# A retention, two mixtures of experts: rows normalised in two pieces, steps of a choice and of an early part placed anew

## The chip, the cores and the metric

The kernel runs on one core of a Trainium2 chip. A core has TensorE (PE, matrix products), VectorE (DVE), ScalarE (ACT) and GpSimd (POOL), SyncE (SP) that issues transfers, and 16 DMA engines. Each engine works through its own instructions in order and waits on semaphores of the others. The metric is the time of one execution on the device in microseconds, as a median of several runs.

## The reference

Three parts follow one another. The first is a causal retention of 8 batches, 8 heads, 576 positions, 64 columns; its output is read as 4608 rows of 512 columns. The second and the third send each row to one of 8 experts of two layers.

```python
scores = scale * np.matmul(q, k.transpose(0, 1, 3, 2))
Dmat = np.where(rel >= 0, gamma[:, None, None] ** rel[None, :, :], 0.0)
x = np.matmul(scores * Dmat[None], v)        # (8, 8, 576, 64), then 4608 rows of 512
...
# first mixture: each row to its best expert, times the gate's probability
expert_idx = np.argmax(x @ w_gate, axis=1)
h = np.maximum(xe @ w1[e], 0.0)              # 512 -> 1024
out[mask] = gate_w[mask, None] * (h @ w2[e]) # 1024 -> 512
...
# second mixture: the pairs (row, expert) by falling logit; a pair is taken
# if its row is free and its expert has fewer than 576 rows
for idx in np.argsort(-flat):
    tok, e = (int(idx) // E, int(idx) % E)
    if assigned[tok] >= 0 or counts[e] >= cap:
        continue
    assigned[tok] = e
    counts[e] += 1
```

## The kernel before, in words

A float32 product is made of float16 products: an operand is split into a high and a low half (w1h and w1l, hh and hl, the two halves of xhl), and three products of halves are summed.

**Attention** (`attention`, L137) goes through 36 row tiles, one in a step, and a list of stages that each step runs for tiles at different offsets. In a step POOL makes qz and vf from the loads of q and v, TensorE makes transposed copies, scores pS and outputs pO, DVE multiplies (s, xT), ACT copies out of PSUM. The small tiles lg, mx, ge, m, OH are the gate's choice for a group of four tiles. Two helper generators are advanced between the stages: `early` at two possible places of a step (`EARLY` lists the pairs of step and place), and `onward`, which holds the setup of later stages; for steps 10 to 17 that is `select_setup` (L1312), in which POOL makes jf and DVE five fsteps out of it.

**early** (L836) prepares the first three row tiles of expert 0 while attention still runs. In its pieces it makes tables, a list, gathers the three tiles (POOL, w2h<-Xs,ix, into a buffer that later holds weights), then for each tile: ACT's Square with a sum into scA, DVE's normaliser on that sum, ACT's Copy with the scale (high half), DVE's low half (w2l<-w2h,scA,w2l), and a transposition issued by SP (xT<-w2l). The first layer of expert 0 starts on these.

**The first mixture** (`moe1`, L1020) runs the experts one after another: `layer1` makes ph in PSUM, ACT evicts hh (L620) and DVE hl (L621), `layer2` makes py. While one expert runs, `prep(e)` (L1042) prepares another in pieces: tables and list, gathers (xg), and for each row tile `normalise` (L550) and `turn`, which issues the transposition xT<-xhl. `normalise` is Square on ACT (L544, or on DVE for expert 0's own rest), the normaliser's three small DVE instructions on sc (L401 to L403), Copy on ACT (L557) and low on DVE (L560). The tile xhl has three buffers. `mixed` advances a piece when the layer has made a given number of matmul calls: `P0`, `N1` and `N6` list these numbers for expert 0, for most of the others and for expert 6, and a dict at L1211 those of expert 0's rest layer. The matmuls, Square and Copy are kept in the order in which they are written; the small DVE instructions follow a scheduler.

**The second mixture** (`moe2`) first makes a choice for each expert: `choose` (L1556) goes through digits of a threshold (cnt, any, dig), then sums what was taken (s on DVE L1615, its matmul L1618), then the base (V, L1670 and L1681) and the list (G, L653 to L655, L676). A choice runs beside the layers of experts chosen earlier. After each of its steps a budget of nanoseconds of matmul columns must have passed before the next one is written; `PACE` holds the budgets for the choices from the fourth on, `FIRST` and `SECOND` those of the first three. From the list follow the gathers xg<-X1s and the transpositions xT<-xg.

Of the kernel before, what the change touches and what calls it, by code (L numbers as in the profile page):

```python
# [9 lines left out]
F32 = mybir.dt.float32  # L10
F16 = mybir.dt.float16
# [5 lines left out]
W = 514  # L17
# [8 lines left out]
TA = 26  # L26
SA = 3
LEAD_IN = 6
CAST = (4, 3)
EARLY = ((28, 1), (29, 0), (29, 1), (30, 0), (30, 1), (32, 0), (32, 1), (33, 0), (33, 1), (34, 0), (34, 1), (35, 0))  # L30
POOL_STORES = 29
AT_GATHER = 30
T0 = (76, 88)
LATE = 4
SOON = 3
P0 = (1, 19, 30, 68, 80)
RANK = (32, 40, 48)
N1 = (14, 82, 102, 122, 142, 170)
LOGITS = (96, 99, 101, 105, 109)
N6 = (30, 50, 70, 90, 108)  # L40
G6 = (102, 114, 184)
G7 = (50, 62, 98, 122, 146, 170)
R = 5
NONE = -1.0e30
LEAD = 2
PACE = dict(key=7000, cnt=3000, any=2000, dig=1800, sum=3300, base=4000, list=3000)
SECOND = dict(key=4000, cnt=2500, any=1700, dig=1500, sum=2600, base=3000, list=2600)
FIRST = dict(key=3000, cnt=1700, any=1200, dig=800, sum=1900, base=3400, list=2600)
ASIDE = dict(key=7500, base=3500, list=4000)
# [485 lines left out]
def scale2(k, x, sc, q, dve=False, pin=False):  # L535

    nc = k.nc
    if dve:
        q = k.fp.tile([128, 512], mybir.dt.bfloat16, name="sq", bufs=1)
        d = nc.vector.scalar_tensor_tensor(q, x, 1.0, x, op0=OP.mult, op1=OP.mult, accum_out=sc[:, 0:1])  # L540
        if pin:
            pe(k, d)
    else:
        d = nc.scalar.activation(q.bitcast(mybir.dt.bfloat16), x, AF.Square, accum_out=sc[:, 0:1])  # L544
        if pin:
            pe(k, d)
    normalizer(nc, sc[:, 0:1], sc[:, 1:2], sc[:, 2:3])


def normalise(k, xg, dve=False, to=None, pin=False):  # L550


    nc = k.nc
    h, sc = to or (k.fp.tile([128, 1024], F16, name="xhl", bufs=3), k.fp.tile([128, 6], F32, name="sc", bufs=12))
    x = xg[:, :512]
    scale2(k, x, sc, h[:, 0:512], dve, pin)
    d = nc.scalar.activation(h[:, 0:512], x, AF.Copy, scale=sc[:, 1:2])  # L557
    if pin:
        pe(k, d)
    nc.vector.scalar_tensor_tensor(h[:, 512:1024], x, sc[:, 1:2], h[:, 0:512], op0=OP.mult, op1=OP.subtract)  # L560
    nc.vector.tensor_scalar(sc[:, 3:4], sc[:, 2:3], 2.0 ** -14, None, op0=OP.mult)
    k.copied = nc.gpsimd.tensor_copy(sc[:, 4:6], xg[:, 512:514])
    return h, sc
# [272 lines left out]
def early(k, X):  # L836


    nc = k.nc
    k.nA = k.cp.tile([128, 4], F32, name="nA")  # L840
    OA = k.OH[:, 0, 0:TA]
    inc = k.lp.tile([128, TA], F16, name="incA", bufs=1)
    nc.vector.tensor_tensor_scan(inc, k.one_h[:, 0:TA], OA, 0.0, op0=OP.mult, op1=OP.add)
    yield
    pb = k.tp([128, 2])
    nc.tensor.matmul(pb[:, 0:1], k.lt_h, inc[:, TA - 1:TA], start=True, stop=True)
    nc.tensor.matmul(pb[:, 1:2], k.one_h, inc[:, TA - 1:TA], start=True, stop=True)
    nc.vector.tensor_copy(k.nA[:, 0:2], pb)
    nc.vector.tensor_tensor(k.nA[:, 2:3], k.nA[:, 0:1], inc[:, TA - 1:TA], op=OP.add)
    nc.vector.tensor_scalar(k.nA[:, 3:4], k.nA[:, 0:1], -1.0, 128.0 * SA, op0=OP.mult, op1=OP.add)  # L850
    yield
    V = k.lp.tile([128, 1, TA + 4], F16, name="VA", bufs=1)
    tables(k, V, TA, inc[:, None, :], k.nA[:, 0:1])
    nc.vector.scalar_tensor_tensor(OA, inc, k.nA[:, 3:4], OA, op0=OP.is_gt, op1=OP.mult)
    begun = cover(k, V[:, 0, :], TA, k.nA[:, 0:1], k.nA[:, 2:3], 128 * SA)
    yield
    ix, _ = lists(k, V[:, 0, :], TA, k.nA[:, 0:1], k.nA[:, 2:3], SA, k.slot, begun=begun)

    yield
    g = k.wp.tile([128, 8, 512], F16, name="w2h").rearrange("p f d -> p (f d)").bitcast(F32)  # L860
    h = k.wp.tile([128, 8, 512], F16, name="w2l").rearrange("p f d -> p (f d)")
    sc = k.cp.tile([128, SA, 6], F32, name="scA")
    rows = [gather(k, X[0:128 * TA, :], ix[:, s:s + 1], xg=g[:, W * s:W * (s + 1)])[:, 0:512] for s in range(SA)]
    to = [h[:, 1024 * s:1024 * (s + 1)] for s in range(SA)]
    k.early = new_xT(k), [sc[:, s, :] for s in range(SA)]

    def square(s):
        nc.scalar.activation(to[s][:, 0:512].bitcast(mybir.dt.bfloat16), rows[s], AF.Square, accum_out=sc[:, s, 0:1])

    def scaled(s):  # L870
        nc.scalar.activation(to[s][:, 0:512], rows[s], AF.Copy, scale=sc[:, s, 1:2])

    def low(s):
        nc.vector.scalar_tensor_tensor(to[s][:, 512:1024], rows[s], sc[:, s, 1:2], to[s][:, 0:512], op0=OP.mult, op1=OP.subtract)
        turn(k, to[s], k.early[0], s)
        nc.gpsimd.tensor_copy(sc[:, s, 4:6], g[:, W * s + 512:W * (s + 1)])

    for s in range(SA):
        yield
        square(s)  # L880
    yield
    normalizer(nc, sc[:, :, 0], sc[:, :, 1], sc[:, :, 2])
    nc.vector.tensor_scalar(sc[:, :, 3], sc[:, :, 2], 2.0 ** -14, None, op0=OP.mult)
    yield
    scaled(0)
    scaled(1)
    yield
    low(0)
    scaled(2)
    yield  # L890
    low(1)
    low(2)


# [121 lines left out]
def moe1(k, X, X1, w1, w2):  # L1016
    nc = k.nc
    X1v = X1.rearrange("(t p) c -> p t c", p=128)
    rows, scales, xTs = {}, {}, {}
    small = lambda e: CAPS[e] == CAP2  # L1020
# [21 lines left out]
    def prep(e):  # L1042

        s0 = 0 if e else SA
        if e == 0:
            yield from moe1_tables(k)
        else:
            xTs[e], scales[e] = new_xT(k), []
        at = args(e)
        n = tiles(e) - s0  # L1050
        begun = cover(*at, CAP2 if small(e) else 128 * n)
        yield
        ix, _ = lists(*at, n, k.slot2 if small(e) else k.slot, small(e), begun=begun)
        rows[e] = [gather(k, X, ix[:, s:s + 1]) for s in range(n)]
        for s in range(n):
            yield
            x, sc = normalise(k, rows[e][s], not e, pin=True)
            turn(k, x, xTs[e], s0 + s, 64 if s == 4 and small(e) else 128)
            scales[e].append(sc)
        for sc in scales[e]:  # L1060
            k.tc.keep_in_program_order(nc.vector.tensor_tensor(sc[:, 0:1], sc[:, 3:4], sc[:, 4:5], op=OP.mult))

# [63 lines left out]
    x1, g, hs, ws, gates = None, {}, {}, {}, {}  # L1126
    for e in range(8):
        w = ws[e] = k.w[e]
        steps = {}
# [43 lines left out]
        to = None  # L1173
# [39 lines left out]
        if e < 6:  # L1213
            x1 = columns(e)
            for s in (4, 0, 1, 2, 3) if small(e) else range(tiles(e)):
                at = {8: load}
                if s == SA and e == 0:
                    steps = {40: load, 20: lambda: next(p1, None), 60: lambda: next(p1, None)}
                    mixed(layer1(k, xTs[0], w, CAP1, to=hs[0], spans=[[(128 * SA, CAPS[0] - 128 * SA)]]), steps)
                if s == (3 if small(e) or e == 5 else tiles(e) - 1) and e < 6:  # L1220
                    ahead = prep(e + 2)
# [90 lines left out]
def select_setup(k):  # L1312
# [36 lines left out]
    for n in range(R):  # L1349
        if n in (2, 4):  # L1350
            yield
        nc.gpsimd.memset(k.f.ones[:, n], 16.0 ** -(n + 1))
        nc.vector.tensor_scalar(k.f.step[:, n], jf, 16.0 ** -(n + 1), None, op0=OP.mult)
    yield
    nc.gpsimd.memset(k.f.ones[0:1], 0.0)
    k.one_f = p.tile([1, 128], F32, name="one_f")
    nc.gpsimd.memset(k.one_f, 1.0)
# [637 lines left out]
```

## Time and profile before

| | us |
|---|---|
| median of three runs | 1047.06 (1047.06 to 1047.94) |
| the profiled execution | 1046.41 |
| its span, first to last instruction | 1044.5 |
| TensorE busy | 998.0 (96%) |
| VectorE busy | 617.6 (59%) |
| ScalarE busy | 441.6 (42%) |
| GpSimd busy | 331.4 (32%) |

Mean granted clock of TensorE over the span: 0.994 of full speed. Attention ends near 194 us, the first mixture near 620, the second's products near 1030; what is behind that are the last stores.

In the timeline a line holds the start, the duration, the engine, the line of the kernel, the operation, what it writes and reads, how many instructions were merged (x3), and in brackets how long the engine had stood idle before and which engine's work released it. L123 is a helper that records all of attention's instructions, so there one goes by the names of tiles. A wait for several semaphores is put down to the one that came last.

### The profile page before, as it was taken

The numbers are of one execution on the slowest core, as the hardware profiler recorded it, in microseconds if no ns is written. First come the engines' busy times: TensorE is split into PE (matmuls) and PEld (weight loads), VectorE is DVE, ScalarE is ACT, GpSimd is POOL, SyncE is SP. The second block draws the span as 40 slices with busy tenths as digits, with TensorE's granted clock in tenths as the row PEclk, the third lists the DMA queues.
The fourth block names the chain that finished last, engine by engine and source line by source line (L and its number), as shares of the span: only waits on it lengthen the run. The fifth ranks groups of instructions, "written<-read, shape, count | busy, mean of one in ns | idle before, by whom it ended". The sixth has DMA issues, their size and how long they took to land.

```text
span 1044.5 us, 23410 instructions
## 1 busy us (share of the span) xinstructions
PE 998.0 (96%) x9165; PEld 665.9 (64%) x9165; DVE 617.6 (59%) x1648; ACT 441.6 (42%) x814; POOL 331.4 (32%) x588
## 2 busy tenths in 40 slices
PE   6999999899999999999999999999999999999994
PEld 5887887556666657565676446474747474757662
DVE  2557767786866566567743676585648475624230
ACT  3556656564545455446521253233223232423330
POOL 6665656431130203030410241523032424313101
PEclk9999999999999999999999999999999999999998
DMA  9899995698887787779972261848274646745510
GB/s 218 204 250 259 236 266 139 155 250 181 203 235 153 213 168 201 175 200 241 197 137 35 72 209 35 231 149 208 77 158 147 153 161 159 215 142 161 142 37 33
DMA packets 276791, 177.65 MB, mean 170 GB/s; under 512 B 201968, under 2 KB 244736, under 8 KB 276672
## 3 DMA queue, kind: packets, MB, share of 16 engines
q1 hardware_dynamic: 264848, 139.22, 55.8%
q0 software_dynamic: 11680, 36.59, 10.8%
q8 instruction: 74, 1.21, 0.5%
q14 instruction: 45, 0.37, 0.1%
q10 hardware_dynamic: 144, 0.26, 0.1%
HBM read 116.83 MB, written 31.02 MB: 142 GB/s over the span
## 4 chain that ended last, share of the span: by engine, by line
PE 71%; DVE 8%; DMA 6%; issue 6%; POOL 4%; ACT 2%; SPq 1%; POOLq 0%; ACTq 0%; DVEq 0%
PE py L641 32%; PE ph L615 28%; PE tp L123 3%; DMA xg<-Xs,ix 2%; PE py L637 2%; PE pO L123 2%; PE pS L123 1%; DMA v<-in_v_dram 1%; POOL vf L123 1%; SPq L123 1%; DVE hl L621 1%; DVE w2l L499 1%; POOL qz L123 1%; DVE w1l L499 1%; DMA xT<-xhl 1%
## 5 line engine op out<-in xcount | busy, mean ns | idle before, releaser
L615 PE MATMUL ph<-xT,w1h 128*128 128x288 f16 (+6 forms) x2048 | 355.4, 289 | 10.7 <-DVE sc L401 3.4
L615 PEld LDWEIGHTS <-w1h 128*128 128x128 f16 x2048 | 195.3, 98 | 69.8 <-issue 15.1
L615 PE MATMUL ph<-xT,w1l 128*128 128x288 f16 (+6 forms) x1024 | 224.7, 289 | 0.0
L641 PE MATMUL py<-w2h,hh 128*128 128x512 f16 x512 | 194.2, 379 | 0.0
L641 PE MATMUL py<-w2h,hl 128*128 128x512 f16 x512 | 194.2, 379 | 0.0
L641 PE MATMUL py<-w2l,hh 128*128 128x512 f16 x512 | 194.1, 379 | 0.0
L641 PEld LDWEIGHTS <-hh 128*128 128x128 f16 x1024 | 98.3, 98 | 109.0 <-issue 0.4
L620 ACT ACTIVATE hh<-ph 128x576 f16<-128x576 f32 (+6 forms) x136 | 80.8, 594 | 171.1 <-PE ph L615 159.6
L621 DVE SCALAR_TENSOR_TENSOR hl<-ph,hh 128x576 f16<-128x576 f32 (+6 forms) x136 | 93.8, 690 | 58.6 <-ACT hh L620 51.7
L615 PEld LDWEIGHTS <-w1l 128*128 128x128 f16 x1024 | 99.6, 98 | 28.2 <-issue 1.7
L499 DVE SCALAR_TENSOR_TENSOR w1l<-stage,w1h 128x1024 f16<-128x1024 f32 x60 | 73.0, 1221 | 41.7 <-ACT w1h L496 40.5
L641 PEld LDWEIGHTS <-hl 128*128 128x128 f16 x512 | 50.1, 98 | 55.9
L499 DVE SCALAR_TENSOR_TENSOR w2l<-stage,w2h 128x1024 f16<-128x1024 f32 x64 | 78.4, 1226 | 8.6 <-ACT w2h L496 8.0
L530 POOL DMA_INDIRECT xg<-X1s,ix x40 | 45.4, 1135 | 107.1 <-DVE ix L685 56.8
L123 DVE TENSOR_TENSOR s<-pS,ct 128x512 f32<-128x512 f32 x72 | 46.4, 686 | 44.7 <-PE pS L123 44.5
L496 ACT ACTIVATE w2h<-stage 128x1024 f16<-128x1024 f32 x64 | 66.8, 1047 | 0.0
L496 ACT ACTIVATE w1h<-stage 128x1024 f16<-128x1024 f32 x60 | 62.2, 1047 | 0.9 <-DMA stage<-in_moe_w_dram 0.9
L544 ACT ACTIVATE x1r<-py 128x512 bf16<-128x512 f32 x37 | 22.0, 596 | 95.5 <-PE py L641 61.3
L698 POOL TENSOR_TENSOR x1r<-nm,sc 128x1 f32<-128x1 f32 x34 | 6.4, 189 | 175.0 <-DVE nm L403 172.6
L123 POOL TENSOR_TENSOR xTl<-xT,xTh 128x512 f16<-128x512 f32 x34 | 39.5, 1163 | 60.6 <-ACT xTh L123 55.5
L530 POOL DMA_INDIRECT xg<-Xs,ix x36 | 41.5, 1152 | 41.2 <-DVE ix L685 25.8
L1775 POOL DMA_INDIRECT out_dram<-w2T,ti x20 | 22.5, 1125 | 92.6 <-ACT w2T L1774 58.7
(399 smaller groups left out, 1507.5 us busy)
## 6 DMA issues: line engine op xcount, KB each, us to landing
stage<-in_moe_w_dram SPq DMA_DIRECT2D x128, 512.0 KB
q<-in_q_dram SPq DMA_DIRECT2D x64, 128.0 KB
k<-in_k_dram SPq DMA_DIRECT2D x32, 256.0 KB
v<-in_v_dram SPq DMA_DIRECT2D x32, 256.0 KB
X1s<-x1r SPq DMA_DIRECT2D x28, 257.0 KB
Xs<-xr SPq DMA_DIRECT2D x5, 1028.0 KB
Xs<-xr POOLq DMA_DIRECT2D x3, 771.0 KB
Xs<-xr POOLq DMA_DIRECT2D x1, 1028.0 KB
```

The lines of the kernel that those rows point to most:

```text
L123: return lambda *args, **kw: self.tc.keep_in_program_order(f(*args, **kw))
L496: d = nc.scalar.activation(at(h, i), t, AF.Copy, scale=128.0)
L499: d = nc.vector.scalar_tensor_tensor(at(l, i), t, 128.0, at(h, i), op0=OP.mult, op1=OP.subtract)
L530: nc.gpsimd.indirect_dma_start(out=xg[:M], out_offset=None, in_=src, in_offset=bass.IndirectOffsetOnAxis(ap=gidx[:M], axis=0))
L544: d = nc.scalar.activation(q.bitcast(mybir.dt.bfloat16), x, AF.Square, accum_out=sc[:, 0:1])
L615: pe(k, nc.tensor.matmul(ph[:, z, :b], x[:, c, F], xT[:, y + c, a:a + b], start=i == 0, stop=i == 11))
L620: nc.scalar.activation(oh, src, AF.Relu)
L621: nc.vector.scalar_tensor_tensor(ol, src, 0.0, oh, op0=OP.max, op1=OP.subtract)
L637: pe(k, nc.tensor.matmul(py[64 * z:64 * z + 64, 0:256], x[:, f, S], y[:, f, 256 * z:256 * z + 256], start=i == 0, stop=i == 23))
L641: pe(k, nc.tensor.matmul(py, x[:, f, S], y[:, f, :], start=i == 0, stop=i == 23))
L698: nc.gpsimd.tensor_tensor(xr[:, 512:513], n[:, 2:3], sc[:, 0:1], op=OP.mult)
L1775: nc.gpsimd.indirect_dma_start(out=out2 if tail else out, out_offset=bass.IndirectOffsetOnAxis(ap=ti, axis=0), in_=y, in_offset=None)
```

## The change

`EARLY` gets two more pairs, (31, 0) and (31, 1); in `early` the three gathers stand in three pieces, the Squares of tiles 1 and 2 in one, and low(1) and low(2) in two. `normalise` is cut in two: `measured` (Square and normaliser) and `scaled` (Copy, low), and `prep` runs `scaled` and `turn` of a tile one piece after its `measured`, just ahead of the next tile's `measured`; so `P0`, `N1` and `N6` get a piece more. In expert 0's rest layer the pieces go from calls 20 and 60 to 24 and 80. In `PACE`, sum goes from 3300 to 4600 and base from 4000 to 5000. In `select_setup` the five fsteps stand together behind the last `yield`.

```diff
-EARLY = ((28, 1), (29, 0), (29, 1), (30, 0), (30, 1), (32, 0), (32, 1), (33, 0), (33, 1), (34, 0), (34, 1), (35, 0))
+EARLY = ((28, 1), (29, 0), (29, 1), (30, 0), (30, 1), (31, 0), (31, 1), (32, 0), (32, 1), (33, 0), (33, 1), (34, 0), (34, 1), (35, 0))
...
-P0 = (1, 19, 30, 68, 80)
+P0 = (1, 19, 30, 68, 80, 92)
...
-N1 = (14, 82, 102, 122, 142, 170)
+N1 = (14, 82, 102, 122, 142, 166, 184)
...
-N6 = (30, 50, 70, 90, 108)
+N6 = (30, 50, 70, 90, 108, 122)
...
-PACE = dict(key=7000, cnt=3000, any=2000, dig=1800, sum=3300, base=4000, list=3000)
+PACE = dict(key=7000, cnt=3000, any=2000, dig=1800, sum=4600, base=5000, list=3000)
...
-def normalise(k, xg, dve=False, to=None, pin=False):
...
+def measured(k, xg, dve=False, pin=False):
+
+    h, sc = k.fp.tile([128, 1024], F16, name="xhl", bufs=3), k.fp.tile([128, 6], F32, name="sc", bufs=12)
+    scale2(k, xg[:, :512], sc, h[:, 0:512], dve, pin)
+    return xg, h, sc, pin
...
+def scaled(k, xg, h, sc, pin):
...
-    rows = [gather(k, X[0:128 * TA, :], ix[:, s:s + 1], xg=g[:, W * s:W * (s + 1)])[:, 0:512] for s in range(SA)]
+    rows = []
+    for s in range(SA):
+        rows.append(gather(k, X[0:128 * TA, :], ix[:, s:s + 1], xg=g[:, W * s:W * (s + 1)])[:, 0:512])
+        yield
...
-    for s in range(SA):
-        yield
-        square(s)
+    square(0)
+    yield
+    square(1)
+    square(2)
...
     low(1)
+    yield
     low(2)
...
-        for s in range(n):
+        for s in range(n + 1):
             yield
-            x, sc = normalise(k, rows[e][s], not e, pin=True)
-            turn(k, x, xTs[e], s0 + s, 64 if s == 4 and small(e) else 128)
-            scales[e].append(sc)
+            if s:
+                x, sc = scaled(k, *m)
+                turn(k, x, xTs[e], s0 + s - 1, 64 if s == 5 and small(e) else 128)
+                scales[e].append(sc)
+            if s < n:
+                m = measured(k, rows[e][s], not e, pin=True)
...
-                    steps = {40: load, 20: lambda: next(p1, None), 60: lambda: next(p1, None)}
+                    steps = {40: load, 24: lambda: next(p1, None), 80: lambda: next(p1, None)}
...
-        nc.vector.tensor_scalar(k.f.step[:, n], jf, 16.0 ** -(n + 1), None, op0=OP.mult)
-    yield
+    yield
+    for n in range(R):
+        nc.vector.tensor_scalar(k.f.step[:, n], jf, 16.0 ** -(n + 1), None, op0=OP.mult)
```

POOL, at the early gathers (w2h<-Xs,ix), near 168 us; before:

```order
155 L123 COPY qz<-q 128x512
156 L123 DMA w2h<-Xs,ix 128x514 x3
157 L123 TENSOR_TENSOR vf<-v,ct 128x512
158 L123 COPY qz<-q 128x512
159 L123 TENSOR_TENSOR vf<-v,ct 128x512
```

and now:

```order
155 L123 COPY qz<-q 128x512
156 L123 DMA w2h<-Xs,ix 128x514
157 L123 TENSOR_TENSOR vf<-v,ct 128x512
158 L123 DMA w2h<-Xs,ix 128x514
159 L123 COPY qz<-q 128x512
160 L123 DMA w2h<-Xs,ix 128x514
161 L123 TENSOR_TENSOR vf<-v,ct 128x512
```

The three gathers, one behind the other before, have one pass of attention between each two.

ACT, in the first layer of expert 2, where `prep` prepares another expert: Square is L544, Copy is L557 before and L566 now, hh is the layer's own eviction. Before:

```order
317 L544 ACTIVATE xhl,sc<-xg 128x512
318 L557 ACTIVATE xhl<-xg,sc 128x512
319 L620 ACTIVATE hh<-ph 128x576
320 L544 ACTIVATE xhl,sc<-xg 128x512
321 L557 ACTIVATE xhl<-xg,sc 128x512
322 L496 ACTIVATE w1h<-stage 128x4x256
323 L620 ACTIVATE hh<-ph 128x576
```

and now:

```order
312 L544 ACTIVATE xhl,sc<-xg 128x512
313 L629 ACTIVATE hh<-ph 128x576
314 L566 ACTIVATE xhl<-xg,sc 128x512
315 L544 ACTIVATE xhl,sc<-xg 128x512
316 L496 ACTIVATE w1h<-stage 128x4x256
317 L629 ACTIVATE hh<-ph 128x576
318 L566 ACTIVATE xhl<-xg,sc 128x512
```

Each Copy stands one eviction further back; the Square stays in its place.

TensorE, at the sum of the fifth choice, beside the layer at 789 us (one_h is the matrix of ones that adds s over the partitions); before:

```order
9801 L615 LDWEIGHTS w1h
9802 L615 MATMUL ph<-xT,w1h 128x288
9803 L1618 LDWEIGHTS one_h
9804 L1618 MATMUL tp<-s_11276,one_h 128x8
9805 L615 LDWEIGHTS w1l
9806 L615 MATMUL ph<-xT,w1l 128x288
```

and now:

```order
9847 L624 LDWEIGHTS w1h
9848 L624 MATMUL ph<-xT,w1h 128x288
9849 L1636 LDWEIGHTS one_h
9850 L1636 MATMUL tp<-s_11291,one_h 128x8
9851 L624 LDWEIGHTS w1h
9852 L624 MATMUL ph<-xT,w1h 128x288
```

The matmul on s stands 46 rows, 23 pairs of weights and matmul, further back.

## Rows read from the trace of the kernel before

**Rows 1.** The page: busy time, share and instructions of each engine.

```profile
PE 998.0 (96%) x9165; PEld 665.9 (64%) x9165; DVE 617.6 (59%) x1648; ACT 441.6 (42%) x814; POOL 331.4 (32%) x588
```

**Rows 2.** Waits of PE, whole span: total us, times, longest.

```profile
PE ph L615 <- DVE sc L401: 3.4, 5, 0.9
...
PE tp L1618 <- DVE s L1615: 1.9, 2, 1.0
PE ph L615 <- DVE sc L403: 1.7, 1, 1.7
PE tp L123 <- DVE st L123: 1.7, 1, 1.7
PE ph L615 <- DMA xT<-w2l: 1.4, 1, 1.4
...
PE tp L1681 <- DVE V L1670: 1.2, 2, 0.7
PE ph L615 <- DVE sc L402: 0.8, 1, 0.8
```

**Rows 3.** Windows: stretch, length, busy by engine, clock, DMA, GB/s.

```profile
195.00:198.50 3.50, 3.50 (x13) 1.68 (x12) 0.92 (x6) 0.56 (x2) 1.77 (x9) 0.51 0.27 101
```

**Rows 4.** Timeline of DVE, then of POOL, 168.5 to 176 us.

```profile
170.45 2.73 DVE L123 TENSOR_TENSOR lg<-lgs 128x32 f32<-128x32 f32 x1
173.21 0.19 DVE L123 TENSOR_REDUCE mx<-lg 128x4 f32<-128x32 f32 x1
...
172.08 1.04 POOL L123 TENSOR_TENSOR vf<-v,ct 128x512 f32<-128x512 f32 x1
```

**Rows 5.** Timeline of DVE, SP and PE, 184 to 204 us.

```profile
187.05 1.41 DVE L123 SCALAR_TENSOR_TENSOR w2l<-w2h,scA,w2l 128x512 f16<-128x512 f32 x2
...
185.92 4.63 SPq L123 DMA_TRANSPOSE xT<-w2l  x3
...
194.44 0.49 PE L615 MATMUL ph<-xT,w1h 128*128 128x384 f16 x2 [1.39 <-DMA xT<-w2l]
...
202.03 0.19 PE L676 MATMUL tp<-nV,G 128*128 128x40 f16 x1 [0.55 <-DVE G L655]
```

**Rows 6.** Timeline of DVE, 82 to 104 us, and of PE.

```profile
87.28 1.36 DVE L123 TENSOR_SCALAR fstep<-jf 128x16 f32<-128x16 f32 x2 [3.46 <-POOL jf L123]
...
101.09 1.29 DVE L123 TENSOR_TENSOR s<-pS,ct 128x512 f32<-128x512 f32 x2 [0.66 <-PE pS L123]
...
89.89 1.16 PE L123 MATMUL pS<-qT,kT 64*128 64x128 f32 x16 [1.18 <-DVE s L123]
```

**Rows 7.** Timeline of ACT and PE, expert 2; waits of PE, 262 to 560 us.

```profile
314.05 0.72 ACT L557 ACTIVATE xhl<-xg,sc 128x512 f16<-128x512 f32 x1 [0.86 <-DVE sc L402]
...
315.62 0.63 ACT L620 ACTIVATE hh<-ph 128x576 f16<-128x576 f32 x1
...
317.69 0.65 PE L615 MATMUL ph<-xT,w1h 128*128 128x288 f16 x4 [0.87 <-DVE sc L401]
318.18 0.29 PE L615 MATMUL ph<-xT,w1l 128*128 128x288 f16 x1
...
PE ph L615 <- DVE sc L401: 2.7, 4, 0.9
```

**Rows 8.** Timeline of ACT and SP, rest layer of expert 0.

```profile
238.63 0.63 ACT L544 ACTIVATE xhl<-xg 128x512 bf16<-128x512 f32 x1 [2.96 <-DMA xT<-xhl]
...
230.06 4.99 SPq L571 DMA_TRANSPOSE xT<-xhl  x2
```

**Rows 9.** Timeline of DVE, PE and SP, 772 to 792 us, beside the fifth choice.

```profile
788.89 0.70 DVE L1615 TENSOR_REDUCE s<-af 128x8 f16<-128x320 f16 x1
...
789.65 0.17 PE L1618 MATMUL tp<-s,one_h 128*128 128x8 f16 x1 [0.99 <-DVE s L1615]
...
773.04 5.72 SPq L571 DMA_TRANSPOSE xT<-xg  x2
...
782.40 0.54 PE L615 MATMUL ph<-xT,w1h 128*128 128x288 f16 x3
```

More of the change, by code (lines that the diff above doesn't have):

```diff
@@ L547, in scale2, with normalise @@
     normalizer(nc, sc[:, 0:1], sc[:, 1:2], sc[:, 2:3])
-def normalise(k, xg, dve=False, to=None, pin=False):
+def measured(k, xg, dve=False, pin=False):
+    h, sc = k.fp.tile([128, 1024], F16, name="xhl", bufs=3), k.fp.tile([128, 6], F32, name="sc", bufs=12)
+    scale2(k, xg[:, :512], sc, h[:, 0:512], dve, pin)
+    return xg, h, sc, pin
+def normalise(k, xg, dve=False):
+    return scaled(k, *measured(k, xg, dve))
+def scaled(k, xg, h, sc, pin):
     nc = k.nc
-    h, sc = to or (k.fp.tile([128, 1024], F16, name="xhl", bufs=3), k.fp.tile([128, 6], F32, name="sc", bufs=12))
     x = xg[:, :512]
-    scale2(k, x, sc, h[:, 0:512], dve, pin)
     d = nc.scalar.activation(h[:, 0:512], x, AF.Copy, scale=sc[:, 1:2])
```

## The prediction

> **What bounds the kernel now.** I read the page first: TensorE is busy for 998.0 us, 96% of the span [rows 1], so no other engine bounds the whole, and what can be won is time in which TensorE stands. The diff adds and removes no matmul, so its busy time stays, unless its clock changes. The waits of TensorE come second [rows 2]; the reader is to see which of them the diff can touch. The largest, on k, is the start of the program and stays. Those on DVE's sc (3.4, 1.7 and 0.8 us), on st (1.7), on the transposed rows xT<-w2l (1.4), on s of the choice (1.9, two times) and on V (1.2, two times), [rows 2] all, stand in stretches that the diff moves. Third comes the clock by windows [rows 3]: behind the last steps of attention the granted clock is 0.51 for 3.5 us, that is the lower of the two levels, 1.2 GHz. It fell after four waits close together, of which the last and longest, 1.39 us, is in [rows 5]. Last I read, around each wait, what stands on the engine that is waited for.
>
> **The change part by part.** All sums go against the profiled execution, 1046.41 us (the span and 1.9 us around it); the median of the three runs is 0.65 us above it, and I add that at the end.
>
> *Gathers of the early rows, one to a step.* Before, POOL issues three gathers in a row, and three elementwise passes (vf, qz, vf) pile up behind them, the last from 172.08 to 173.12 [rows 4]. DVE's small lg starts at 170.45 and takes 2.73 us, to 173.18, where mx behind it, as small, takes 0.19: it ends as POOL's passes end. Behind lg stand s and st, and TensorE waits 1.7 us for st [rows 2]. After, the gathers stand between the passes, so lg meets one pass, 1.04 us at most, instead of three. I take 1.5 of the 1.7 us (bounds 0, if one pass is enough to delay s as far, and 1.7). The gathers stay three and on POOL.
>
> By the Trainium skill, GPSIMD Engine Reference, 1. Specifications, GpSimd shares its SBUF interfaces with VectorE, with contention for VectorE instructions that read two SBUF inputs or run in a two-port mode. The row on lg, which has two such inputs, agrees. By that rule alone a lg beside one pass would still lose up to 1.04 us, and the sum would be some 0.5 us lower.
>
> *The early tiles' pieces closer.* The squares of tiles 1 and 2 stand together, both Copies too, and low(0) and low(1) each come one piece earlier. SP issues the three transpositions from 185.92 on in 4.63 us, and TensorE waits 1.39 us for the last [rows 5]. DVE's lows set when SP may issue. Low(2) stays in its step, but low(1) no longer stands in front of it (two lows took 1.41 us [rows 5], so half, 0.7), and SP has done the second transposition a piece earlier. With 0.7 us won at least I take 1.1 of the 1.39 (bounds 0 and 1.39).
>
> *The clock.* If two of the waits before 195 go or shrink, it may not fall. 3.50 us at 0.51 hold 1.75 us of work at the full clock; this is the upper bound. But TensorE then comes sooner to a wait that DVE's chain sets (on G, 0.55 us at 202.03 [rows 5]), and that wait grows. I take 1.0 (bounds 0 and 1.75). The three shorter waits in front of it stay, so this is the least certain term.
>
> The Trainium skill, TensorE: Matmul & The Clock Gate, The HAM clock gate, says that the throttled clock is the default and that activity releases it. The drop behind four waits agrees. By it alone, with the largest of the four gone, the clock would hold and the sum would be 0.75 us higher.
>
> *fstep in one place.* Before, DVE stands 3.46 us until POOL has made jf, then two fsteps take 1.36 us, s comes behind them, and TensorE waits 1.18 us for it [rows 6]. After, no fstep stands there; s can follow its pS. At the new place five fsteps (at 0.19 us each, as mx, 0.95) stand in front of an s before which DVE idles 0.66 us [rows 6]: 0.3 us at most. The gain is 1.2 less 0.3, 0.9 (bounds 0, if the next waits take it back, and 1.2).
>
> *Rows normalised in two pieces.* ACT's Copy, DVE's low and the transposition come one piece later than Square and the normaliser. So an hh of the layer, which stood behind a Copy that waits for sc, now stands ahead of it. The first layer of expert 2 shows it [rows 7]: ACT's Copy waits 0.86 us, hh comes at 315.62 only, and TensorE waits 0.87 us at 317.69. In experts 1 to 6 there are five waits on sc, four of 2.7 us in all [rows 7] and the one of 0.8 [rows 2]: 3.5 us. Replaying expert 2 with the durations of its rows in the new order, the 0.87 us become about 0.2, since hh is evicted before Copy; but low then stands in front of other evictions. I take 2.0 (bounds 0 and 3.5). What it costs: no instruction is added. The last tile's transposition comes 14 calls later, 1.7 us at 0.12 us a call (four from 317.69 to 318.18 [rows 7]); its reader is the first layer of the next expert, a whole second layer later, which is cover enough.
>
> In the rest layer of expert 0 ACT's Square stands 2.96 us until a transposition frees a buffer of xhl, hh is queued behind it, and TensorE waits 1.7 us for sc L403 [rows 2, 8]; with another 0.7 on sc (3.4 less 2.7 [rows 2, 7]) that is 2.4 us. The pieces go from calls 20 and 60 to 24 and 80: the later Square comes up to 2.4 us later (20 calls), nearly when its buffer is free. In return the low of the tile before can stand in front of an hl. I take 1.0 (bounds -1.5, a wait on low as long as the one lost on Square, and 2.4).
>
> *The choice's last sums later.* In two choices TensorE reaches the matmul on s before DVE has made s: 0.99 us at 789.65 [rows 9], 0.9 in the next, 1.9 in all; V adds 0.7 in a third [rows 2]: 2.6 us. s starts at 788.89 and takes 0.70. The matmul moves behind 23 more matmuls of 288 columns, 2.8 us, so that wait goes. The price: the choice's list comes later too, by 1.3 us in the fourth choice and by up to 5 in a later one, and with it the gathers and transpositions of the next expert's rows, and on SP the load of the expert's number moves behind stage loads. For the rows of the fourth, SP is done with the last transposition at 778.76, and the layer that reads it starts at 782.40 without a wait [rows 9]. The nearest row from SP done to released is xT<-w2l, 190.55 to 194.44, 3.9 us [rows 5]; by it there is no margin, and the 1.3 us could show in full. I take 0.3. 2.4 less 0.3 is 2.1 (bounds -1.0, with 1.3 us late in three choices, and 2.6).
>
> The sum: 1.5 + 1.1 + 1.0 + 0.9 + 2.0 + 1.0 + 2.1 = 9.6 us. 1046.41 less 9.6 is 1036.8, with 0.65 for the median 1037.5; I give 1037.5.
>
> **The rivals.** *xhl becomes the bound (slower).* There are three buffers. With the split, a tile's transposition is issued a piece later, while the Square that takes its buffer again stays: two pieces, 40 calls or 4.9 us, lie between instead of three. Copy, low and SP's issue take some 2 of these, so Square waits if the transposition lands more than 3 us after its issue. One issued from 230.06 freed its buffer only at 238.6 [rows 8]. Then hh stands behind Square and TensorE behind hh, 1.7 us a time by that case. Without the two split terms 6.6 us of gain are left, so from four or five such waits on the kernel is slower; at one in each of six experts it is 1047.06 - 6.6 + 10.2 = 1050.7. For it: that row, and no buffer is added. Against it: this wait is by far the longest of its kind, though the buffers are as many elsewhere.
>
> *Only the places of the waits change.* low in front of hl costs what sc cost, the list is late by its whole shift and the clock falls all the same: 1.5 + 1.1 + 0.9 + 1.3 = 4.8 us, 1042.3. For it: DVE is busy beside every eviction. Against it: hh no longer waits.
>
> *It doesn't do what it says.* lg still meets a pass that delays s, and lists come 1.3 us late in four experts: 1.1 + 0.9 + 2.0 + 1.0 + 2.6 - 5.2 = 2.4 us, 1044.7.
>
> **How the numbers follow.** Forecast, the seven terms in about these sizes, 1034 to 1040: 0.56. The second and third rivals, 1040 to 1045: 0.25. xhl or late lists as the bound, above 1045: 0.16, half of it slower. Upper bounds met at once, below 1034: 0.03. The range 1034 to 1045 leaves 0.19 out. About 0.2%, 2.1 us, can be told from no change: faster (below 1045.0) 0.84, within 0.09, slower 0.07.
>
> **What would show it.** Right: no wait of TensorE on st near 174 nor on s near 90; lg at 0.2 us; clock 1.0 from 195 on; no Square waiting for xT<-xhl; no wait on the choice's s. Wrong: waits on hl, or on transposed rows, rise by what those on sc lose; the clock still at 0.5 from 195; xT<-xg new among the waits after 780.

## The result, and the profile after

The changed kernel takes 1035.08 us in the median of four executions (1033.35 to 1035.14); the ratio to the kernel before is 0.9868, 95% interval 0.9852 to 0.9884. Of the 1047.06 us before, that ratio makes 1033.2 us, a gain of 13.8 us where 9.6 were forecast; a second comparison, below, gave 0.9851. The direction was right. The range began at 1034 and the time by the ratio lies 0.8 us under it: the gain was sized too small. The median of the four executions themselves, 1035.08, lies inside the range; what lies outside is the gain against the kernel before.

The page after, its span and the busy time of each engine:

```profile
span 1031.6 us, 23405 instructions
PE 994.1 (96%) x9165; PEld 665.1 (64%) x9165; DVE 616.3 (60%) x1648; ACT 441.3 (43%) x814; POOL 334.3 (32%) x588
```

As many matmuls as in [rows 1], in a span that is 12.9 us shorter. TensorE's waits after (total, times, longest):

```profile
PE tp L123 <- DMA k<-in_k_dram: 8.2, 2, 7.1
PE ph L624 <- DVE hl L630: 4.5, 6, 1.2
...
PE ph L624 <- ACT xr L123: 0.9, 1, 0.9
PE tp L123 <- DVE st L123: 0.8, 1, 0.8
PE tp L1604 <- DVE cmp L1598: 0.7, 1, 0.7
...
PE tp L755 <- DMA w2T<-w2l: 0.5, 1, 0.5
...
PE tp L1699 <- DVE fnr L1660: 0.4, 1, 0.4
```

Of [rows 2], all waits on sc (5.9 us), on s of the choice, on xT<-w2l, and half of that on st are gone. New are one on xr, one on cmp, one on fnr and one on w2T, late in the first mixture; those on hl are the largest that can be touched.

Where the time went is read by laying the same matmul of both traces side by side: how far ahead TensorE is after each place, and what that place added.

| matmul at (before, after) | us ahead | added there | forecast |
|---|---|---|---|
| pO behind fstep's place, 91.30, 89.33 | 1.97 | 1.9 from 82 on | 0.9 |
| tp<-ct,xT behind st, 175.21, 171.28 | 3.93 | 2.0 | 1.5 |
| first matmul of expert 0, 194.44, 189.75 | 4.69 | 0.75 | 1.1 |
| the same layer, 198.34, 192.02 | 6.31 | 1.6, the clock | 1.0 |
| rest layer of expert 0, 241.68, 232.68 | 9.00 | 2.7 | 1.0 |
| experts 1 to 6, 535.37, 524.03 | 11.34 | 2.3 | 2.0 |
| the choices, 895.50, 882.30 | 13.21 | 1.9 | 2.1 |

At three of the places the timelines after read as follows (start, length, engine, line, operation; in brackets the idle time before and its releaser), DVE and PE near 169 us, then PE in the rest layer and in expert 2:

```profile
168.65 0.59 DVE L123 TENSOR_TENSOR lg<-lgs 128x32 f32<-128x32 f32 x1
...
171.28 0.66 PE L123 MATMUL tp<-ct,xT 128*128 128x128 f32 x4 [0.82 <-DVE st L123]
...
228.09 0.35 PE L624 MATMUL ph<-xT,w1h 128*128 128x224 f16 x2 [1.09 <-DVE hl L630]
...
311.31 0.65 PE L624 MATMUL ph<-xT,w1h 128*128 128x288 f16 x4 [0.97 <-DVE hl L630]
```

lg, 2.73 us in [rows 4], takes 0.59. The wait on sc of [rows 7] is gone, but a new one on hl of the same size stands four us further on, and one of 1.09 us in the rest layer, in place of the waits there of 1.7 and 0.7.

### The profile page after: what moved, and what is told of

Same layout as the page of the kernel before. It is cut to its first block, busy times and chain, and to the rows that moved or that the text cites. A ratio compares the mean times of both kernels' runs of the same rounds, so it can differ in the third digit from the quotient of the medians.

```text
span 1031.6 us, 23405 instructions
## 1 busy us (share of the span) xinstructions
PE 994.1 (96%) x9165; PEld 665.1 (64%) x9165; DVE 616.3 (60%) x1648; ACT 441.3 (43%) x814; POOL 334.3 (32%) x588
## 3 DMA queue, kind: packets, MB, share of 16 engines
q8 instruction: 74, 1.21, 0.5%
## 4 chain that ended last, share of the span: by engine, by line
PE 74%; DVE 7%; DMA 5%; issue 5%; POOL 3%; ACT 3%; SPq 1%; POOLq 0%; ACTq 0%; DVEq 0%
PE py L650 31%; PE ph L624 30%; PE tp L123 4%; PE py L646 2%; PE pO L123 2%; PE pS L123 2%; DMA stage<-in_moe_w_dram 1%; POOL qz L123 1%; POOL vf L123 1%; DVE hl L630 1%; DVE w2l L499 1%; DMA xT<-xhl 1%; DMA v<-in_v_dram 1%; DMA xg<-Xs,ix 1%; SPq L123 1%
## 5 line engine op out<-in xcount | busy, mean ns | idle before, releaser
L624 PE MATMUL ph<-xT,w1h 128*128 128x288 f16 (+6 forms) x2048 | 353.7, 288 | 5.9 <-DVE hl L630 4.5
L624 PEld LDWEIGHTS <-w1h 128*128 128x128 f16 x2048 | 195.3, 98 | 63.1 <-issue 7.2
L624 PE MATMUL ph<-xT,w1l 128*128 128x288 f16 (+6 forms) x1024 | 223.6, 288 | 0.0
L624 PEld LDWEIGHTS <-w1l 128*128 128x128 f16 x1024 | 99.4, 98 | 27.2 <-issue 0.6
L544 ACT ACTIVATE x1r<-py 128x512 bf16<-128x512 f32 x37 | 22.1, 597 | 92.3 <-PE py L650 56.1
```

The source lines that it names most:

```text
L624: pe(k, nc.tensor.matmul(ph[:, z, :b], x[:, c, F], xT[:, y + c, a:a + b], start=i == 0, stop=i == 11))
```

## The experiments

Each part of the change was put alone into the kernel before; single edits followed. "Ahead" is again by the same matmul, against the profile before or, where said, against one of the changed kernel.

**The five fsteps alone.**

```diff
-        nc.vector.tensor_scalar(k.f.step[:, n], jf, 16.0 ** -(n + 1), None, op0=OP.mult)
-    yield
+    yield
+    for n in range(R):
+        nc.vector.tensor_scalar(k.f.step[:, n], jf, 16.0 ** -(n + 1), None, op0=OP.mult)
```

> The kernel before with the five fsteps at their new place alone. Theory (each part takes away the waits at its own place, whatever the others do): the wait of 1.18 us on s at 90 and the two of 0.2 to 0.3 beside it go, TensorE is 2.0 us ahead from 92 us on, and the time falls by 2.0 us; the clock still drops at 195 and everything behind keeps its waits. Rival (the gain was taken back further on, or belongs to the other parts): under 0.9 us.

Ratio 0.9983 (0.9972 to 0.9995), 1.8 us. TensorE is 2.6 us ahead at 91.30, of which 0.7 stem from the start of the program. That leaves 1.9: 0.24 at a matmul at 88.06 us and 1.6 behind it. No cost shows at the new place, where DVE still idles before s:

```profile
97.76 0.47 DVE L123 TENSOR_SCALAR fstep<-jf 128x16 f32<-128x16 f32 x5
98.50 1.29 DVE L123 TENSOR_TENSOR s<-pS,ct 128x512 f32<-128x512 f32 x2 [0.26 <-PE pS L123]
```

In this profile the clock is at its lower level from 191 to 198 us and again from 239.

**The wait or the work?** The fsteps stay, jf comes a step earlier.

```diff
     nc.gpsimd.memset(k.f.nr, -float(CAP2))
+    jf = p.tile([128, 16], F32, name="jf16")
+    nc.gpsimd.iota(jf, pattern=[[1, 16]], base=0, channel_multiplier=0, allow_small_or_imprecise_dtypes=True)
     yield
...
-    jf = p.tile([128, 16], F32, name="jf16")
-    nc.gpsimd.iota(jf, pattern=[[1, 16]], base=0, channel_multiplier=0, allow_small_or_imprecise_dtypes=True)
```

> The kernel before with POOL's iota for jf one step earlier, the fsteps where they were. Theory (it is the wait for jf in front of s, not the five small instructions): the wait on s at 90 goes all the same, 1.6 to 2.0 us at 92. Rival (the work itself, beside POOL's vf, delays s): the fsteps still take over 1 us and TensorE still waits for s, under 0.6 us.

The wait on s goes all the same: 1.6 us between 88 and 91.3, ratio 0.9986 (0.9974 to 0.9998). DVE's timeline of this kernel:

```profile
83.56 0.24 DVE L123 TENSOR_SCALAR fstep<-jf 128x16 f32<-128x16 f32 x2
84.40 1.29 DVE L123 TENSOR_TENSOR s<-pS,ct 128x512 f32<-128x512 f32 x2 [0.60 <-PE pS L123]
...
87.11 1.21 DVE L123 TENSOR_SCALAR fstep<-jf 128x16 f32<-128x16 f32 x2
89.28 1.29 DVE L123 TENSOR_TENSOR s<-pS,ct 128x512 f32<-128x512 f32 x2 [0.97 <-PE pS L123]
```

The first pair, with jf ready, takes 0.24 us, where it took 1.36 in [rows 6]. The second pair does take 1.21 us, beside a pass of POOL, and costs nothing, since s waits for pS 0.97 us longer. So it was the wait for jf, and where the passes stand against it.

**The early part alone, and its gathers alone.** The first run has both hunks on `early`; the second leaves the squares, Copies and lows where they were. Both have the two new pairs in `EARLY`. Of the second:

```diff
-    rows = [gather(k, X[0:128 * TA, :], ix[:, s:s + 1], xg=g[:, W * s:W * (s + 1)])[:, 0:512] for s in range(SA)]
+    rows = []
+    for s in range(SA):
+        rows.append(gather(k, X[0:128 * TA, :], ix[:, s:s + 1], xg=g[:, W * s:W * (s + 1)])[:, 0:512])
+        yield
```

> The kernel before with the early part alone (gathers apart, pieces closer). Theory of independent parts: lg takes under 0.3 us, the wait on st falls from 1.70 to 0.8 us and the two short stops before it go (2.0 us in all), the last transposition comes 0.75 us sooner against TensorE, and the clock stays at 1.0 at 195 (1.6 us): 4.3 us, or 2.7 if the clock drops all the same. Rival (the clock held only because other waits in attention went too): the clock at 0.5 for 3 us in this profile and 2.7 us.

> The kernel before with the three early gathers in three pieces; squares, normaliser, Copies and lows stay where they were. Theory (the pile of POOL's passes makes lg slow): lg under 0.3 us, the wait on st at 175 falls from 1.70 to 0.8 us, the short stops before it go, 2.0 us; the transposition is as late as before, 1.4 us, and the clock may drop at 195 as before. Rival (lg is slow for another reason, or the pieces' places matter more than the gathers): under 0.5 us until 180.

Ratios 0.9954 (0.9935 to 0.9972) and 0.9963 (0.9947 to 0.9979). In both TensorE gains 2.0 us between 170 and 176. DVE, then PE of the kernel with the gathers alone:

```profile
170.22 0.59 DVE L123 TENSOR_TENSOR lg<-lgs 128x32 f32<-128x32 f32 x1
170.84 0.19 DVE L123 TENSOR_REDUCE mx<-lg 128x4 f32<-128x32 f32 x1
...
172.84 0.66 PE L123 MATMUL tp<-ct,xT 128*128 128x128 f32 x4 [0.81 <-DVE st L123]
```

lg takes 0.59 us, not under 0.3 as expected: in the changed kernel POOL's qz lies beside it until 169.20, and lg ends at 169.24. With the pile gone the 2.73 us are 0.59, and one pass still costs 0.4 us. With the gathers alone the first layer starts no earlier against TensorE than before; with the pieces closer it starts 1.28 us earlier, behind a wait of 0.36 us on lgs, and the clock is 1.00 from 189 to 196 in that profile (PE, then the window, with the columns of [rows 3]):

```profile
190.61 0.48 PE L615 MATMUL ph<-xT,w1h 128*128 128x384 f16 x2 [0.36 <-ACT lgs L123]
```

```profile
189.00:196.00 7.00, 5.72 (x41) 3.34 (x41) 5.67 (x21) 4.52 (x13) 3.38 (x11) 1.00 0.52 187
```

The clock did not need the other parts to hold there. It does not hold in every execution: the mean clock was 0.996 in two of the seven executions of this kernel and 0.991 to 0.994 in the others.

By the Trainium skill, GPSIMD Engine Reference, 1. Specifications, VectorE's instructions with two SBUF inputs or in a two-port mode contend with GpSimd. lg beside qz agrees; the fsteps, which read one tile, were slowed as well (1.21 us against 0.24), so two inputs alone don't tell which instruction is slowed; whether the fsteps run in a two-port mode no run here shows.

**The cut in two alone, and the calls of the rest layer.** The second run is the changed kernel with the old calls, the third the kernel before with the new calls and nothing else.

```diff
-                    steps = {40: load, 20: lambda: next(p1, None), 60: lambda: next(p1, None)}
+                    steps = {40: load, 24: lambda: next(p1, None), 80: lambda: next(p1, None)}
```

> The kernel before with rows normalised in two pieces alone, with the calls 24 and 80. Theory of independent parts: 2.7 us in expert 0's rest layer and 2.3 us in experts 1 to 6, 5.0 us in all, no wait of Square on xT<-xhl over 0.5 us. Rival (part of the 2.7 came from the earlier arrival of TensorE and of the transfers in the whole change): under 3.8 us, with Square waiting for a transposition in the rest layer.

> The changed kernel with the pieces of expert 0's rest layer at calls 20 and 60 again. Theory (the later calls let the transposition free its buffer): Square waits some 2 us for xT<-xhl again and 1.5 to 2.5 of the 2.7 us in that layer are lost. Rival (the cut in two did it, the calls matter little): the rest layer within 0.7 us of the changed kernel.

> The kernel before with the calls 24 and 80 in expert 0's rest layer, and no cut in two. Theory (the later calls free Square of the transposition by themselves): Square's wait of 2.96 us at 238 falls under 0.7 us and 1.5 to 2.0 us are won in that layer. Rival (it takes both edits, since an uncut piece at call 80 puts the wait for sc in front of a later hh): under 0.8 us won.

The cut alone, with the calls: ratio 0.9952 (0.9936 to 0.9969), 5.0 us; TensorE gains 2.8 us in the rest layer and 2.3 from there to 536. Square waits 3.9 us for xT<-xhl there, in five places and up to 1.4, where I expected none over 0.5. The changed kernel with the old calls loses 1.8 us of the rest layer against the changed one (ratio 0.9862, 0.9843 to 0.9880, against 0.9851 of the changed kernel in the same call). The new calls without the cut win 2.4 us there, ratio 0.9958 (0.9941 to 0.9974). ACT, PE of the kernel with the old calls, then ACT of the one with the new calls alone:

```profile
233.67 0.63 ACT L544 ACTIVATE xhl<-xg 128x512 bf16<-128x512 f32 x1 [1.49 <-DMA xT<-xhl]
...
235.11 0.35 PE L624 MATMUL ph<-xT,w1h 128*128 128x224 f16 x2 [1.64 <-DVE sc L402]
```

```profile
235.91 0.36 ACT L620 ACTIVATE hh<-ph 128x224 f16<-128x224 f32 x1 [1.09 <-PE ph L615]
237.53 0.36 ACT L620 ACTIVATE hh<-ph 128x224 f16<-128x224 f32 x1 [1.26 <-PE ph L615]
238.63 0.63 ACT L544 ACTIVATE xhl<-xg 128x512 bf16<-128x512 f32 x1 [0.75 <-DMA xT<-xhl]
```

With the old calls Square waits and hh stands behind it, with or without the cut. With the new ones two more hh pass first (235.91 and 237.53), and Square starts at 238.63, no earlier than in [rows 8], though TensorE was 0.85 us ahead in this profile (that the two agree to the hundredth is chance): the transposition came no sooner, and what stood behind Square has moved. Of the 2.8 us in that layer the two numbers of calls did 1.8 to 2.4; the cut with the old calls makes the other 1.0.

**The budgets alone, and larger.**

```diff
-PACE = dict(key=7000, cnt=3000, any=2000, dig=1800, sum=3300, base=4000, list=3000)
+PACE = dict(key=7000, cnt=3000, any=2000, dig=1800, sum=4600, base=5000, list=3000)
```

> The kernel before with the two larger budgets alone. Theory of independent parts: the waits on s at 789 and 835 and on V at 886 go (2.7 us), new waits of 0.7 us on cmp and 0.4 on fnr come in the later choices: 1.9 us. Rival (the lists come too late when nothing ahead has changed): a wait on xT<-xg at 782 of up to 1.3 us, and under 1 us in all.

> The changed kernel with the budgets sum 5900 and base 6000 in place of 4600 and 5000. It prices lateness of the choice. Theory (the lists have room left, and the sums wait no more): within 0.7 us of the changed kernel. Rival (there is no room behind the list): waits on xT<-xg at the starts of the last layers, 1.3 us or more in each of one to four of them.

Alone: ratio 0.9985 (0.9971 to 0.9999), 1.6 us. PE's waits of that kernel from 740 to 1010 us, where before there were 1.9 on s, 0.7 on V and 0.2 on G:

```profile
PE tp L1586 <- DVE cmp L1580: 0.7, 1, 0.7
PE tp L1681 <- DVE fnr L1642: 0.4, 1, 0.4
```

No wait on xT<-xg appears, so the feared late list isn't there. With 5900 and 6000 the changed kernel takes 1034.97 us, ratio 0.9874 (0.9858 to 0.9891). The same stretch then has waits of 0.9 us on G and 0.8 on r, and TensorE falls 1.4 us back against the second profile of the changed kernel between 525 and 890 us. The time lies within 0.7 us of the changed kernel's, as the theory had it, but the sums do wait, and no layer waits for xT<-xg, as the rival had it: the transpositions come in time even so, but a step moved further meets the next work that isn't ready.

**Two buffers of xhl.** It prices the rival that would have made the change slower.

```diff
-    h, sc = k.fp.tile([128, 1024], F16, name="xhl", bufs=3), k.fp.tile([128, 6], F32, name="sc", bufs=12)
+    h, sc = k.fp.tile([128, 1024], F16, name="xhl", bufs=2), k.fp.tile([128, 6], F32, name="sc", bufs=12)
```

> The changed kernel with two buffers of xhl in place of three. It prices the rival of the prediction, that Square waits for a transposition, with hh behind it. Theory (a transposition lands some 3 us after its issue, so two buffers are too few and three just enough): Square waits over 2 us in most tiles of experts 1 to 6, and 10 to 30 us are lost. Rival (there was plenty of room): under 3 us lost.

1051.36 us, ratio 1.002 (1.0008 to 1.0033): some 18 us are lost, all of the gain and more. ACT's wait of this kernel, then the same wait of the changed kernel:

```profile
ACT xhl L544 <- DMA xT<-xhl: 24.1, 11, 6.6
```

```profile
ACT xhl L544 <- DMA xT<-xhl: 3.2, 5, 1.1
```

The rival's mechanism is real and one buffer away. With three it shows as 3.2 us of ACT in five places (3.4 in three in the kernel before, 2.96 of it in [rows 8]), and one of these, 0.29 us at 308.9, is part of the wait of 0.97 us in expert 2.

**One eviction between each two pieces.** Evictions come every 24 calls; the list of pieces had two between 120 and 144.

```diff
-N1 = (14, 82, 102, 122, 142, 166, 184)
+N1 = (14, 82, 102, 126, 150, 172, 188)
```

In the second run, also:

```diff
-                    steps = {40: load, 24: lambda: next(p1, None), 80: lambda: next(p1, None)}
+                    steps = {40: load, 36: lambda: next(p1, None), 84: lambda: next(p1, None)}
```

> The changed kernel with the pieces of a prepared expert at calls 14, 82, 102, 126, 150, 172 and 188, so that one eviction of the layer lies between each two from 102 on (evictions come every 24 calls). Theory (the waits on hl that are left in experts 1 to 6, 0.49, 0.97 and 0.3 us, come from two pieces between one pair of evictions): the wait of 0.97 us in expert 2 goes, 1.0 to 1.5 us between 250 and 520 us. Rival (low on DVE stands in front of hl wherever the piece is): the same waits at other groups, within 0.5 us.

> As the one before, and the pieces of expert 0's rest layer at calls 36 and 84 in place of 24 and 80. Theory (the 1.09 us on hl at 228 stand behind the low of the output rows and that of the piece, both between the first two evictions): some 0.8 us less in that layer. Rival (the piece at 36 delays its transposition, so that the next Square waits for its buffer): Square's wait for xT<-xhl over 1 us and nothing won.

1032.97 us, ratio 0.9847 (0.9831 to 0.9862), and 1032.26, ratio 0.9845 (0.983 to 0.9861). PE's waits from 200 to 520 us in the changed kernel, then with the pieces spread:

```profile
PE ph L624 <- DVE hl L630: 3.1, 4, 1.1
```

```profile
PE ph L624 <- DVE hl L630: 1.7, 2, 1.1
```

TensorE gains 1.7 us between 250 and 500 against the changed kernel's first profile, and the wait of 0.97 us is not there. One profile tells little here, since these waits change from one execution to the next: the changed kernel's 0.97 us in expert 2 are missing in the profile with the larger budgets, whose code is the same up to there. So I counted all stops of TensorE over 0.08 us between 246 and 540 us in every profile: 3.3 to 5.6 us in nine with rows normalised in one piece, 1.1 to 2.5 in five with the cut and the change's list, 0.8 and 0.7 with the pieces spread, and 1.9 in a third kernel that has them spread, below. The new place in the rest layer wins 1.0 and gives 0.9 back one eviction later, so it is no gain of its own. By their medians the two are 1 to 3 us under the changed kernel; the intervals of the ratios overlap.

**jf earlier, with the pieces spread; the early part with the fsteps' new place.** In the changed kernel the first layer of expert 0 waits 0.89 us for xr, with the early part alone 0.36 us for lgs. The first of these two kernels is the one with the pieces spread and the edit on jf above in place of the fsteps' new place; the second is the kernel before with both other hunks and no more.

> The changed kernel with the pieces spread (14, 82, 102, 126, 150, 172, 188), and with jf made one step earlier in place of the fsteps' new place. Theory (the new place of the fsteps lengthens the wait before expert 0's first layer from 0.36 to 0.89 us): that wait is 0.36 us on lgs again, the clock stays at 1.0 there, and the time is 0.5 to 2 us under that of spread. Rival (other parts of the change do it): 0.89 us on xr as in spread, and the same time.

> The kernel before with the early part and the fsteps' new place, nothing else. Theory (the fsteps' new place lengthens the wait before expert 0's first layer): 0.89 us on xr. Rival (the cut in two or the budgets do it): 0.36 us on lgs, as with the early part alone.

1033.0 us, ratio 0.9852 (0.9836 to 0.9868), and 1041.22, ratio 0.9934 (0.9919 to 0.9949). PE's wait is the same in both; the line is that of the second, the first has it under L624:

```profile
PE ph L615 <- ACT xr L123: 0.9, 1, 0.9
```

So the fsteps' hunk, put to the early part, brings the longer wait, and jf made earlier brings it as well. Why a step at 87 us changes for which eviction the layer waits 100 us later was not found: between 150 and 190 us TensorE and ACT do the same work in the same order with and without it. The layer's PSUM buffers are my guess, not shown. It costs 0.5 us, and in both profiles the clock falls at that place, as it does not in the profile with the early part alone.

**Both kernels once more, for the clock.**

> The changed kernel once more, for its time in more executions and for its clock. Theory (the two kernels differ in how often the clock drops, beside the waits): the mean granted clock of the executions is 0.995 without and 0.993 to 0.994 with one stretch at the lower level, the times fall in steps of about 1.7 us, and no drop comes at 175 us or in the rest layer of expert 0. Rival (the clock is as it was in the one profile): all executions near 1033.4 with 0.995.

> The kernel before once more, for the clock. Theory (its waits of 1.70 us at 175, of 1.39 us at 194 and of 1.73 us at 240 each let the clock drop in some executions, and the one profile had one drop of up to three): a mean clock of 0.989 to 0.993 over the executions, and in this profile stretches at 0.5 at two or three of these places. Rival (the profile before was typical, one drop at 195): one drop, and a mean of 0.994 in most executions.

The changed kernel: 1034.36 us, ratio 0.9851 (0.9836 to 0.9867). The kernel before: 1048.73, ratio to itself 0.9999. Windows (start and end, length, busy time by engine, clock, DMA share, GB/s) of the profiled execution of this second run of the kernel before, of the changed kernel's first profile, and of its second:

```profile
175.50:179.00 3.50, 3.50 (x52) 2.94 (x50) 1.63 (x5) 2.21 (x9) 2.55 (x3) 0.51 0.02 5
196.00:199.50 3.50, 3.50 (x13) 1.63 (x12) 1.05 (x6) 0.93 (x2) 1.78 (x9) 0.51 0.28 106
```

```profile
189.00:192.50 3.50, 2.75 (x17) 1.75 (x18) 2.50 (x13) 1.53 (x7) 0.39 (x2) 1.00 0.59 226
```

```profile
188.50:192.00 3.50, 3.12 (x11) 1.56 (x12) 2.20 (x11) 0.55 (x3) 0.77 (x2) 0.51 0.52 199
```

The kernel before has a second stretch at the lower level here, behind the wait on st, that its first profile [rows 3] did not have. The changed kernel has one at the end of attention in its second profile and none in its first. And the budgets alone, with all of attention and of the rest layer as before, had three:

```profile
174.90:178.30 3.40, 3.40 (x39) 2.82 (x40) 1.82 (x6) 2.57 (x9) 1.96 (x3) 0.50 0.02 5
195.40:198.80 3.40, 3.40 (x13) 1.62 (x11) 1.13 (x5) 0.15 (x1) 1.77 (x9) 0.50 0.26 99
243.20:246.60 3.40, 3.40 (x16) 2.10 (x16) 0.78 (x2) 1.08 (x3) 0.00 (x0) 0.50 1.17 265
```

Over 100 executions of the kernel before, beside all these kernels, the mean granted clock is 0.988 to 0.994, 0.992 in the median, and the time 1045.4 to 1052.4, 1048.9 in the median; the 0.994 of its first profile is the best of them, reached by four. The changed kernel in eight executions: 0.993 to 0.995 and 1033.4 to 1035.1. My expectation of steps of 1.7 us in its times fits the first four of these, and not the second four, which all have 0.993.

The second profile of the kernel before also has a wait that the first showed small. PE at the first layer of expert 6, the first profile, then the second:

```profile
524.00 0.70 PE L615 MATMUL ph<-xT,w1h 128*128 128x320 f16 x4 [0.31 <-DVE hl L621]
```

```profile
526.55 0.70 PE L615 MATMUL ph<-xT,w1h 128*128 128x320 f16 x4 [1.50 <-DVE hl L621]
```

The kernels with the fsteps, the budgets, the gathers, jf and the new calls alone, whose rows are normalised in one piece too, have 1.3 to 1.5 us there, the early part alone 1.2, and the early part with the fsteps 0.2. So seven of nine profiles have 1.2 us or more, and the first was a lucky one.

## Why the prediction fell short

Most of the mechanisms were right, and all but two terms were sized too small. The largest misses are the rest layer of expert 0 (1.0 forecast, 2.7 measured), fstep (0.9 and 1.9) and the clock (1.0 and 1.6, for other drops than those I had in mind).

**Gathers apart** (1.5, measured 2.0): right in its mechanism, and shown by the run with nothing else. Beside the wait on st, two stops of TensorE of 0.2 and 0.4 us just before it went too, which I had not counted.

**Pieces closer** (1.1, measured 0.75): the wait on xT<-w2l is gone, and a wait of 0.9 us on xr, the last eviction of attention, stands in its place, 0.36 on lgs with the early part alone. I named no follower for that wait; the follower set the gain.

**The clock** (1.0, measured 1.6 in the first pair of profiles): the step that failed is that one profile stood for the kernel. The clock fell at 195 there, and I asked only whether that drop would go. In the second profile of the kernel before it falls behind the wait on st too, and in three kernels with the same rest layer behind the wait there. The profiles bear out which wait goes with which drop: the kernels that keep a wait of 1.6 us or more on st have the drop at 175 in four of six further profiles, those with 0.8 us there in none of eleven. A drop near 240 was seen in three of nine profiles with the old calls and three buffers, and in none of the eight with new ones, which points the same way but is few. The drop at the end of attention, which I thought gone, is there in seven of eight profiles of the changed kernel and its variants; the first of them, without it, was luck. So the term was sized on the wrong drops: what went, as far as these profiles show, are those behind st and in the rest layer, and the one that I counted on mostly stays.

**fstep** (0.9, measured 1.9, and 1.8 by the ratio of the run alone): two parts of this term failed. I left out the two short stops beside the wait on s, 0.24 us before it and 0.3 on xT behind it, and I charged 0.3 us at the new place, where no cost shows.

**Rows in two pieces** (2.0, measured 2.3): right, with the exchange that I feared, sc for hl, at less than half the size. The count over the profiles says the same: the middle one is 4.4 us in one piece and 2.3 in two.

**The rest layer** (1.0, measured 2.7): the largest miss. I took a value in the middle between -1.5 and 2.4, since low might stand in front of hl. It does, 1.09 us, but in an earlier group. The rows had what was needed: Square had to wait until 238.6 whatever its place, and evictions in front of it would be free. That is the upper bound of 2.4 and not the middle, and the two runs on the calls show it. Three short waits on hl in that layer, 0.2 to 0.3 us each, went too; I had not counted them.

**The choice** (2.1, measured 1.9, 1.6 by the ratio of the run alone): right, though the price was another. The lists are not late; the matmuls moved further on meet cmp and fnr.

**The rivals.** xhl did not become the bound, by one buffer. The waits' places did change in part, for 4.5 us on hl in place of 3.1. No list came late.

The four parts alone make 1.8, 4.8, 5.0 and 1.6 us by their ratios, 13.2 in sum, against 13.8 and 15.6 of the whole in its two comparisons: within their intervals the parts neither help nor hinder one another; by trace one pair does, by the 0.5 us on xr. By the trace the sum of forecasts lacks 3.5 us, of which the rest layer makes 1.7, fstep 1.0, the clock 0.6 and the gathers 0.5, less 0.35 and 0.2 at the pieces and the choice, with 0.3 more in experts 1 to 6.

What stays open: why the fsteps' hunk lengthens the wait on xr, how often each drop comes, and whether the remaining one at the end of attention would go with that wait or needs the three short ones before it to go.

## What to carry to other kernels

Where an instruction waits for a transfer in front of an eviction on the same engine, put it behind the eviction: in the rest layer the transfer landed no earlier, but what had stood behind the instruction moved, and 2.4 us were won. Where a buffer's cycle is the limit, count what one buffer fewer would cost before the work is cut in more pieces. A profile is one execution: take a second one before a term is sized on a clock drop or on a single wait.

## What the runs showed of the hardware

The lower level of TensorE's clock came behind single waits of 2.5 us and less amid dense work, in some executions and not in others: on st it came behind 1.76, 1.76, 1.77 and 2.38 us and not behind 1.62, 1.63 and 1.70; in the rest layer with three buffers, behind 2.30, 2.42 and 2.50 and not behind 1.64 to 2.13. So the length of the wait alone does not decide. Such a stretch cost 1.5 us behind st and 1.6 at the end of attention.

DVE instructions of 128x16 and 128x32 elements took 0.24 us for two (fstep) and 0.18 to 0.19 for one (mx) with no pass beside them, and 1.21 (two) and up to 2.73 us (lg) beside POOL's elementwise passes, until the pass or the pile of passes ended. lg in [rows 4] began 0.07 us before the first of three passes (170.52) and ended 0.06 behind the last. Not every small instruction is slowed. DVE and POOL in the profile before:

```profile
82.79 0.19 DVE L123 TENSOR_REDUCE m<-ge 128x4 f32<-128x32 f32 x1
83.01 0.71 DVE L123 TENSOR_TENSOR OH<-ge,m 128x32 f16<-128x32 f32 x1
...
82.63 1.04 POOL L123 TENSOR_TENSOR vf<-v,ct 128x512 f32<-128x512 f32 x1
```

There the reduction m took 0.18 and 0.19 us beside vf (two places) and the reciprocal gt 0.18 beside vf or qz (seven), while OH and ge, with two inputs, took 0.71 to 0.78 beside vf (five). A gather on POOL beside DVE's xTl slowed nothing: 0.69 us at 169.84, as at 192.04, where POOL issued a store.
